# Lightning attention, a Fourier mix and an MLP on one core: two planner costs raised, behind a norm and behind a fold

## The chip, the cores and the metric

The kernel runs on one core of a Trainium2 chip. The metric is the device time of one execution in microseconds; the time of a kernel is the median of several runs on the chip. A profiled execution is recorded apart, and its times of single instructions are quoted here with the line of the kernel that issued them (L644 is line 644).

## The reference

Four batches of 768 tokens, eight heads of 64, so 512 features. Causal linear attention with a decay per head, in blocks, is followed by a Fourier mix over tokens and features, a layer norm, and an MLP of 512 to 2048 to 512. All is float32.

```python
intra = einsum('bhic,bhjc->bhij', qb, kb) * Dmask
out[:, :, sl] = einsum('bhij,bhjd->bhid', intra, vb) + einsum('bhid,bhde->bhie', qb * lam_pow, kv_state)
kv_state = lam_block * kv_state + einsum('bhsd,bhse->bhde', kb * rev_pow, vb)
...
x = attention.transpose(0, 2, 1, 3).reshape(4, 768, 512)
u = x + real(fft(fft(x, axis=1), axis=2))
un = (u - mean(u)) / sqrt(var(u) + 1e-6)
return u + relu(un @ w_ch1) @ w_ch2
```

## The kernel before

**Groups.** A batch is six tiles of 128 tokens. The Fourier mix is symmetric, so tile t is always finished with its mirror tile t + 3; such a pair is a group (b, g), 256 tokens. There are twelve groups in the order `ORDER`: for each batch g = 1, 2, 0. The first four, (0,1), (0,2), (0,0) and (1,1), are `PLAIN`: their MLP is computed directly. The other eight are `LATE`; they are taken in pairs by a scheme with fewer products (`late`, L891 and on), which begins when everything else is done, at about 425 us, and runs to the end.

**The front work of a batch.** `attn(b)` goes through six chunks of 128 tokens. Each loads k, q and v (L265, queue of SyncE), transposes k and q on TensorE (L276, L281), forms the scores (L300), masks them with the decay on VectorE (L304), updates the state (L320, L322), forms the output (L335, L341) and turns it back (L357); ScalarE empties that turn in two copies (L361, L362). The rows needed in mirrored order are written to DRAM (L376 for the last ones, on ScalarE's queue) and gathered back by GpSimd (L448, L461). Then `fft_ln(b)` does the mix. `fold_a` and `fold_b` add and subtract mirrored rows and columns on VectorE (L435 to L439, then L479 to L493); the token transform follows on TensorE (L525, the first of which is pinned to its place in the program), then for each t = 1, 2, 0 the feature transform (`width`, L537 to L542), its assembly on VectorE (L607 to L611) and `norm`: statistics on VectorE (L554, L555), two small operations on GpSimd (L558, L559), the normalised tokens `un` on VectorE (L572). For a plain group TensorE transposes `un` into `ut` (L577); for a late group VectorE transposes it (L585) and it is stored in DRAM (L589), with the unnormalised tokens (L595).

**The other work.** `mlp` is cut into chunks: for each of the 16 column blocks `fc` four matmuls of 256 columns (L644), each a pair of records in the trace, into one of three PSUM banks `pm`, and a ReLU that frees the bank. The ReLU stands on ScalarE (L652), but in the second half of the blocks every odd one stands on VectorE (L650). Behind the blocks come the matmuls of 512 columns of the second layer (L658), and their sums with the tokens (L665 to L670 on VectorE). `half[0]` holds the first eight blocks of the first three plain groups, `half[1]` the other eight; the fourth plain group is one `mlp` of all sixteen. The conversion of the weights from 8-byte words (`load_weights`, L211 to L227) is a third kind of work, and the sums of weights for the late stage (`combine_weights`, L709 on VectorE) a fourth.

**What sets the order.** All pieces are generators that yield an estimated cost. `weave(lead, other, ratio)` takes a piece of the lead, adds its cost, and then takes pieces of the other work until their costs reach `ratio` times the lead's. The front work is the lead and MLP blocks are the other work. So the number that a front piece yields sets how much other work is written behind it in the program; a scheduler then orders each engine's instructions, and each engine runs its own list in that order. When `fft_ln` of the fourth batch is done, what is left of the MLP of (1,1) is woven with the sums of weights, and then the late stage starts with `inputs(0)` (L792 to L798), which stands behind the MLP's last sums in VectorE's list.

```python
def weave(lead, other, ratio):
    t_lead = t_other = 0.0
    for d in lead:
        t_lead += d
        while t_other < t_lead * ratio:
            d = next(other, None)
...
run(weave(fr, back, (t_back - t_half) / (t_rest - t_rest * t_half / t_back)))
...
load_u(0, nc.scalar)
run(weave(combine_weights(0), back, 1.5))
run(back)
```

`LEADS` is (0,): the first batch's mix is written in single pieces, and the branch of `fft_ln` that runs the folds as a whole, with a fixed cost behind each, serves batches 1, 2 and 3.

Of the kernel before, what the change touches and what calls it, by code (L numbers as in the profile page):

```python
# [76 lines left out]
def kernel(  # L77
# [61 lines left out]
    def new(pool, shape, tag, **kw):  # L139
        cnt[0] += 1  # L140
        return pool.tile(shape, F32, tag=tag, name=f"{tag}{cnt[0]}", **kw)

    def psum_a(shape):
        return new(pa, shape, "pa")
# [112 lines left out]
    LEADS = (0,)  # L257
# [207 lines left out]
    def fold_a(b):  # L465
        for a, n in enumerate(BLK):
            yield from fold_x(b, a, n, 1, eo[b][a][1][0:n, 1, 0:DM], xn_[b, HC + a][0:n])
# [32 lines left out]
    def fft_ln(b):  # L500
        sets = []

        def piece(a, i, n):

            c0 = W + QM if i == 4 else QM * (i % 2)
            return sets[a][i in (2, 3)][0:BLK[a], n, c0:c0 + QM]

        if b in LEADS:
            yield from fold_a(b)
            yield from fold_b(b, sets)  # L510
            yield 2.0
        else:
            yield 1.0
            run(fold_a(b))
            yield 6.0 if b - 1 in LEADS else 3.0
            run(fold_b(b, sets))
            yield 12.0 if b - 1 in LEADS else 9.0


        for i in range(5):  # L520
            ps = psum_a([128, 2, NK])
            m = 128 if i < 4 else 1
            for n in range(2):
                for a, rows in enumerate(BLK):
                    mm = nc.tensor.matmul(ps[:, n, :], lhsT=piece(a, i, n), rhs=cs[0:rows, a, i in (2, 3), n, :],  # L525
                                          start=(a == 0), stop=(a == 1))
                    if i + n + a == 0:
                        tc.keep_in_program_order(mm)
            nc.scalar.copy(ys[i][0:m, 0:2 * NK].rearrange("p (k n) -> p n k", n=2), ps[0:m])
            yield 1.4  # L530


        def width(t, ps, only_a):
            y = [ys[i][:, S // 2:S // 2 + 1].broadcast_to([128, 128]) if only_a else ys[i][:, 128 * t:128 * t + 128] for i in range(5)]
            mm = nc.tensor.matmul
            if not only_a:
                mm(ps[:, HM + QM:DM], lhsT=y[2], rhs=dt[:, 2, 0:QM], start=True, stop=True)  # L537
            mm(ps[:, HM:HM + QM + 1], lhsT=y[0], rhs=dt[:, 0, :], start=True, stop=False)
            mm(ps[:, HM:HM + QM + 1], lhsT=y[4], rhs=dt[:, 4, :], start=False, stop=True)
            mm(ps[:, 0:QM], lhsT=y[1], rhs=dt[:, 1, 0:QM], start=True, stop=True)  # L540
            if not only_a:
                mm(ps[:, QM:HM], lhsT=y[3], rhs=dt[:, 3, 0:QM], start=True, stop=True)  # L542

        def even_odd(t):
            return t.rearrange("p (m r) -> p r m", r=2)

        def halves(t):
            return t.rearrange("p (r k) -> p r k", r=2)

        def norm(g):  # L550
            mv = new(np_, [128, G, 2], "mv")
            for i in range(G):
                stt = new(np_, [128, 6], "stt")
                nc.vector.bn_stats(stt, xs[b, TT[g][i]])  # L554
                nc.vector.bn_aggr(mv[:, i, :], stt)  # L555
            ve = new(np_, [128, G], "ve")
            rs = new(np_, [128, G], "rs")
            nc.gpsimd.tensor_scalar(ve, mv[:, :, 1], EPS, None, op0=ALU.add)  # L558
            nc.gpsimd.tensor_tensor(rs, ve, mhalf, op=ALU.pow)  # L559

            yield 9.0 if (b, g) == PLAIN[0] else 1.0
            plain = (b, g) in PLAIN
            if plain:
                ut = uts[b, g] = new(up, [128, KO, G * 128], "ut")
            else:

                to = utd[b, g] = dram.tile([128, KO, G * 128], F32, name=f"utd{b}{g}")
            for i in range(G):
                un = new(np_, [128, DM], "un", bufs=1)
                u = xs[b, TT[g][i]]  # L570
                for o, x in ((un[:, 0:HM], u[:, 0:HM]), (un[:, HM:DM], u[:, DM - 1:HM - 1:-1])):
                    nc.vector.tensor_scalar(o, x, mv[:, i, 0:1], rs[:, i:i + 1],  # L572
                                            op0=ALU.subtract, op1=ALU.mult)
                if plain:
                    pt = psum_a([128, KO, 128])
                    for c in range(KO):
                        mm = nc.tensor.transpose(pt[:, c, :], un[:, 128 * c:128 * c + 128], ident)  # L577
                        if (b, g, i, c) == (*PLAIN[0], 0, 0):

                            tc.keep_in_program_order(mm)  # L580
                    nc.scalar.copy(ut[:, :, 128 * i:128 * i + 128], pt)
                else:

                    uq = new(ep, [128, DM], "e")
                    nc.vector.transpose(uq, un)  # L585
                    for r in range(0, 128, 32):
                        dst = to[:, :, 128 * i + r:128 * i + r + 32].rearrange("(a d) c n -> d c a n", d=32)
                        src = uq[r:r + 32].rearrange("p (c a n) -> p c a n", c=KO, n=32)
                        nc.sync.dma_start(dst, src)  # L589
                yield 0.7  # L590
            if plain:
                return
            for T in TT[g]:
                ud[b, T] = dram.tile([128, DM], F32, name=f"ud{b}{T}")
                nc.sync.dma_start(ud[b, T], xs.pop((b, T)))  # L595

        for t in (1, 2, 0):
            ps = psum_a([128, DM])
            width(t, ps, False)

            A = halves(ps)[:, ::-1, 0:QM]
            B = bs[t % 2]
            nc.scalar.copy(B[:, 1:HM:2], ps[:, QM:HM])
            nc.scalar.copy(B[:, 2:HM:2], ps[:, HM + QM + 1:DM])
            ds = new(fp, [128, 2 * (HM + 2)], "ds")
            nc.scalar.copy(ds[:, HM:2 * HM + 2:HM + 1], ps[:, HM + QM:HM + QM + 1].broadcast_to([128, 2]))
            nc.vector.tensor_tensor(even_odd(ds[:, 0:HM]), A, even_odd(B[:, :]), op=ALU.subtract)  # L607
            nc.vector.tensor_tensor(even_odd(ds[:, HM + 1:2 * HM + 1]), A, even_odd(B[:, :]), op=ALU.add)
            u, v_ = xs[b, t], xs[b, HC + t]
            nc.vector.tensor_tensor(halves(u), halves(u), halves(ds)[:, :, 0:HM], op=ALU.add)  # L610
            nc.vector.tensor_tensor(halves(v_), halves(v_), halves(ds[:, 1:DM + 1])[:, ::-1, :], op=ALU.add)  # L611
            yield 1.6
            if t == 0:
                ps = psum_a([128, DM])
                width(HC, ps, True)
                x3 = xn_.pop((b, HC))
                nc.vector.tensor_tensor(even_odd(v_[0:1, 0:HM]), halves(ps[0:1])[:, ::-1, 0:QM],
                                        even_odd(x3[0:1, 0:HM]), op=ALU.add)
                nc.vector.tensor_tensor(v_[0:1, HM:DM:2], ps[0:1, 0:QM], x3[0:1, HM:DM:2], op=ALU.add)
                nc.vector.tensor_tensor(v_[0:1, HM + 1:DM:2], ps[0:1, HM + 1:HM + QM + 1],  # L620
                                        x3[0:1, HM + 1:DM:2], op=ALU.add)
                yield 0.9
            yield from norm(t)
# [3 lines left out]
    PLAIN, LATE = ORDER[:4], ORDER[4:]  # L627
# [543 lines left out]
    def front(b):  # L1171
        yield from attn(b)
        yield from fft_ln(b)
# [15 lines left out]
    def run(gen):  # L1189
        return sum(gen)  # L1190
# [18 lines left out]
    def beside(lead, t, other, t_other):  # L1209
        return weave(lead, part(other, t_other), t_other / t)  # L1210

    att1, mix = attn(1), fft_ln(0)
    att0 = attn(0)
    run(part(att0, 2.7))
# [4 lines left out]

    half = [[mlp(b, g, h * FO // 2, (h + 1) * FO // 2) for b, g in PLAIN[:3]] for h in range(2)]  # L1220
    fr = chain([att1, fft_ln(1)] + [front(b) for b in range(2, B)])
    t_rest, t_back = 3 * t_front - 5 * t_chunk, len(PLAIN) * t_mlp - 50.0
    t_half = 1.5 * t_mlp
# [49 lines left out]
```

## Time and profile before

| | us |
|---|---|
| median of 3 runs | 794.67 (794.67 to 795.24) |
| profiled execution | 796.12 |
| its span | 793.9 |
| TensorE idle in the span, 0 to 103 | 15.4 |
| 103 to 148 | 2.1 |
| 148 to 258 | 1.0 |
| 258 to 366 | 3.5 |
| 366 to 428 | 0.3 |
| 428 to the end | 8.2 |

The rows of idle time are the width of a stretch less TensorE's busy time in it, from the table of windows. The stretch from 103 to 428 us is the one in which front work and MLP are woven; the late stage is the last. In the profile a group of like instructions stands on one line: start, duration, engine, line, operation, output and inputs by the program's names, shape, number of records, and in brackets the idle time before it with what ended it. The granted clock is full (1.00) in every one of these stretches but the last two, 0.97 from 366 to 428 and 0.99 after.

### The profile page before, as it was taken

The page shows a single profiled execution, that of the slowest core. Times are in us where ns is not written, and L with a number is a line of the kernel's source. Part 1 is how long each engine was busy: PE and PEld are TensorE (multiplying, and loading weights), DVE is VectorE, ACT ScalarE, POOL GpSimd, SP SyncE. Part 2 cuts the span into 40 slices and gives each one's busy share as a digit, 9 for nine tenths or more (in the row PEclk, how much of TensorE's full clock was granted, in tenths as well). Part 3 has the DMA queues.
Part 4 walks back from the last instruction along what each step waited for, and adds up shares of the span by engine and source line. Part 5 has one row for each costly group of instructions (what it writes and reads, how often), then busy time and mean ns, then how long its engine had stood idle before and what let it go on. Part 6 is the DMA issues. An engine that isn't in the chain of part 4 may idle for free.

```text
span 793.9 us, 14617 instructions
## 1 busy us (share of the span) xinstructions
PE 763.4 (96%) x5616; PEld 646.3 (81%) x5616; DVE 585.5 (74%) x1148; ACT 225.4 (28%) x532; POOL 197.6 (25%) x198
## 2 busy tenths in 40 slices
PE   6889989999999999998999999999999999999995
PEld 5768766758585867767946889988999999999995
DVE  6899889675844582345698998769966699758983
ACT  3665443335621221321201221022211342034300
POOL 3223330011111110211004950279205001220021
PEclk9999999999999999999999999999999999999998
DMA  9978723238842147441233374345944455455341
GB/s 243 247 165 245 196 85 129 85 74 205 227 116 77 54 79 146 108 143 64 54 66 107 133 246 162 97 167 191 348 147 153 150 174 185 129 176 186 121 131 70
DMA packets 152331, 116.80 MB, mean 147 GB/s; under 512 B 113998, under 2 KB 113998, under 8 KB 152262
## 3 DMA queue, kind: packets, MB, share of 16 engines
q1 hardware_dynamic: 147120, 103.39, 45.8%
q0 software_dynamic: 2112, 6.69, 2.4%
q10 hardware_dynamic: 3030, 5.78, 2.0%
q8 instruction: 45, 0.74, 0.4%
q14 instruction: 24, 0.20, 0.1%
HBM read 83.58 MB, written 32.25 MB: 146 GB/s over the span
## 4 chain that ended last, share of the span: by engine, by line
PE 78%; DVE 9%; DMA 4%; issue 4%; ACT 1%; POOL 1%; SPq 0%; POOLq 0%; ACTq 0%; DVEq 0%
PE p L1046 21%; PE p L891 12%; PE p L976 11%; PE pm L658 10%; PE pm L644 9%; PE pa L525 3%; PE pa L300 3%; PE pa L341 3%; DMA x<-xb,ix 2%; PE pa L335 2%; PE pa L276 1%; PE pa L357 1%; PE pa L320 1%; DVE sc L304 1%; PE pa L281 1%
## 5 line engine op out<-in xcount | busy, mean ns | idle before, releaser
L644 PE MATMUL pm<-ut,w 128*128 128x256 f32 x512 | 119.7, 384 | 0.0
L658 PE MATMUL pm<-w,hr 128*128 128x512 f32 x256 | 115.7, 596 | 0.2 <-DVE w L227 0.2
L644 PEld LDWEIGHTS pm<-ut,w 128*128 128x128 f32 x512 | 95.6, 192 | 14.2 <-issue 2.1
L658 PEld LDWEIGHTS pm<-w,hr 128*128 128x128 f32 x256 | 46.6, 190 | 49.3 <-issue 48.0
L1060 POOL TENSOR_TENSOR y<-y,u 128x512 f32<-128x512 f32 x12 | 18.8, 1569 | 199.2 <-DVE y L1069 156.8
L1046 PE MATMUL p<-tx,sx 128*128 128x128 f32 x416 | 54.9, 275 | 0.0
L1046 PEld LDWEIGHTS p<-tx,sx 128*128 128x128 f32 x416 | 50.6, 192 | 0.0
L891 PE MATMUL p<-ur,w 128*128 128x256 f32 x192 | 46.9, 379 | 0.1
L272 POOL TENSOR_TENSOR kd<-k,decay 128x512 f32<-128x512 f32 x20 | 22.0, 1100 | 95.3 <-PE pa L320 48.7
L1052 ACT COPY y<-p 128x128 f32<-128x128 f32 x48 | 12.8, 266 | 104.1 <-PE p L1046 103.8
L1054 DVE TENSOR_TENSOR y<-p,y 128x128 f32<-128x128 f32 x92 | 25.5, 286 | 22.5 <-PE p L1046 15.9
L891 PEld LDWEIGHTS p<-ur,w 128*128 128x128 f32 x192 | 36.3, 190 | 5.7 <-issue 0.5
L304 DVE TENSOR_TENSOR sc<-pa,decay 128x512 f32<-128x512 f32 x48 | 31.5, 683 | 8.1 <-PE pa L300 7.9
L1046 PE MATMUL p<-w,ha 128*128 128x128 f32 x288 | 37.4, 275 | 0.0
L300 PEld LDWEIGHTS pa<-qT,kT 64*128 64x128 f32 x384 | 26.1, 193 | 13.4 <-ACT qT L283 7.4
L652 ACT ACTIVATE hr<-pm 128x256 f32<-128x256 f32 x44 | 16.7, 385 | 66.2 <-PE pm L644 66.0
L1046 PEld LDWEIGHTS p<-w,ha 128*128 128x128 f32 x288 | 35.0, 192 | 0.2
L300 PE MATMUL pa<-qT,kT 64*128 64x128 f32 x384 | 30.8, 292 | 3.3 <-ACT qT L283 3.1
L341 PE MATMUL pa<-sc,v 128*64 128x128 f32 x384 | 30.0, 279 | 4.0 <-DVE sc L304 3.8
L558 POOL TENSOR_SCALAR ve<-mv 128x2 f32<-128x2 f32 x12 | 3.4, 286 | 122.3 <-DVE mv L555 122.3
L891 PE MATMUL p<-sx,w1s 128*128 128x256 f32 x128 | 32.9, 380 | 0.2 <-DVE sx L794 0.2
L650 DVE TENSOR_SCALAR hr<-pm 128x256 f32<-128x256 f32 x20 | 8.3, 414 | 32.8 <-PE pm L644 32.8
(234 smaller groups left out, 1736.6 us busy)
## 6 DMA issues: line engine op xcount, KB each, us to landing
tx<-td SPq DMA_DIRECT2D x84, 256.0 KB, 2.7
raw<-in_moe_w_ch_dram SPq DMA_DIRECT2D x32, 512.0 KB, 4.0
tx<-sd SPq DMA_DIRECT2D x42, 256.0 KB, 2.7
sd<-tx SPq DMA_DIRECT2D x28, 256.0 KB, 2.1
k<-in_k_dram SPq DMA_DIRECT2D x24, 256.0 KB, 5.2
q<-in_q_dram SPq DMA_DIRECT2D x24, 256.0 KB, 4.3
v<-in_v_dram SPq DMA_DIRECT2D x24, 256.0 KB, 5.0
td<-tx SPq DMA_DIRECT2D x21, 256.0 KB, 2.0
```

The source lines that it names most:

```text
L272: nc.gpsimd.tensor_tensor(kd, kt, kpow, op=ALU.mult)
L300: mm(pss[hi][:, hp, :], lhsT=kT[HD[hi], hp, :], rhs=qT[HD[hi], hp, :], start=True, stop=True)
L304: nc.vector.tensor_tensor(t, pss[hi], decay[:, hi::2, :], op=ALU.mult)
L341: mm(po[HD[hi], hp, :], lhsT=vt[:, 2 * hp + hi, :], rhs=sc[hi][:, hp, :], start=(c == 0 and hp == 0), stop=(hp == HP - 1), skip_group_chec ...
L525: mm = nc.tensor.matmul(ps[:, n, :], lhsT=piece(a, i, n), rhs=cs[0:rows, a, i in (2, 3), n, :], start=(a == 0), stop=(a == 1))
L644: nc.tensor.matmul(ps, lhsT=w1[:, c, 128 * fc:128 * fc + 128], rhs=ut[:, c, :], start=(c == 0), stop=(c == KO - 1))
L658: nc.tensor.matmul(ps, lhsT=hr[(fc - f0) // 4][:, fc % 4, 128 * i:128 * i + 128], rhs=w2[:, fc, :], start=(fc == f0), stop=(fc == f1 - 1))
L891: nc.tensor.matmul(ps, lhsT=s2.A[a][:, kt, 128 * i:128 * i + 128], rhs=U[b][:, kt, :], start=(first and kt == 0), stop=(kt == 1), skip_gro ...
L976: nc.tensor.matmul(ps[:, 128 * i:128 * i + 128], lhsT=ab[m][0][:, 128 * i:128 * i + 128], rhs=ab[m][1], start=(start and i == 0), stop=Tru ...
L1046: nc.tensor.matmul(ps[:, 0:HM // 2], lhsT=ab[m][0][i], rhs=ab[m][1][:, i, :], start=(start and i == 0), stop=(i == HF // 2 - 1), skip_grou ...
L1054: V.tensor_tensor(o, ps[:, 0:HM // 2], o, op=ADD)
L1060: nc.gpsimd.tensor_tensor(o, y, u, op=ADD)
```

## The change

Two of the yielded costs are changed, and nothing else. In `fft_ln`, the cost behind `fold_b` is raised from 9.0 to 11.5 for the batches that are not below `LATE[-1][0]`, which is 3: so for batch 3 alone. Batch 1 keeps 12.0 and batch 2 keeps 9.0. In `norm`, the cost between the statistics and the normalised tokens is raised from 1.0 to 3.0 for the plain groups other than the first, that is (0,2), (0,0) and (1,1). The line that sets `plain` moves up since the new cost uses it.

```diff
             run(fold_b(b, sets))
-            yield 12.0 if b - 1 in LEADS else 9.0
+            yield 12.0 if b - 1 in LEADS else 9.0 if b < LATE[-1][0] else 11.5
...
-            yield 9.0 if (b, g) == PLAIN[0] else 1.0
             plain = (b, g) in PLAIN
+            yield 9.0 if (b, g) == PLAIN[0] else 3.0 if plain else 1.0
             if plain:
                 ut = uts[b, g] = new(up, [128, KO, G * 128], "ut")
```

## The prediction

> **What bounds the kernel now.** I read the busy table first, then the timeline of TensorE for its idle places, then, around each of those that the change can reach, the timeline of VectorE and the chain of waits, and last the TensorE windows of 1 us, for the granted clock.
>
> ```profile
> span 793.9 us, 14617 instructions
> PE 763.4 (96%) x5616; PEld 646.3 (81%) x5616; DVE 585.5 (74%) x1148; ACT 225.4 (28%) x532; POOL 197.6 (25%) x198
> 147.16 0.76 PE L577 MATMUL pa<-ident,un 128*128 128x128 f32 x4 [0.94 <-DVE un L572]
> 176.14 1.69 PE L300 MATMUL pa<-qT,kT 64*128 64x128 f32 x16
> 257.72 0.90 PE L525 MATMUL pa<-cs,fe 128*128 128x193 f32 x4 [0.98 <-DVE fe L484]
> 292.07 1.09 PE L341 MATMUL pa<-sc,v 128*64 128x128 f32 x16 [1.23 <-DVE sc L304]
> 365.64 0.59 PE L525 MATMUL pa<-cs,fe 128*128 128x193 f32 x2 [2.04 <-DVE fe L484]
> 427.76 1.10 PE L891 MATMUL p<-sx,w1s 128*128 128x256 f32 x4 [0.22 <-DVE sx L794]
> ```
>
> TensorE is busy 96% of the span, so only its 30.5 us of idle (793.9 - 763.4) and its clock can be won without removing work. The number in brackets is the idle time before the group and what ended it. The reader is to see that every one of these waits on VectorE, at a seam between two batches, and that the largest is at the fourth batch's folds (365.64). There the windows give a second cost (columns: width, busy and matmuls, granted clock, DMA share, GB/s):
>
> ```profile
> 365.00:366.00 1.00, 0.36 (x2) 1.00 0.00 0
> 366.00:367.00 1.00, 1.00 (x5) 0.56 0.00 0
> 367.00:368.00 1.00, 1.00 (x4) 0.50 0.06 16
> 368.00:369.00 1.00, 1.00 (x4) 0.50 0.00 0
> 369.00:370.00 1.00, 1.00 (x4) 0.73 0.00 0
> 370.00:371.00 1.00, 1.00 (x6) 1.00 0.00 0
> ```
>
> After the 2.04 us hole the clock is halved: 0.44 + 0.50 + 0.50 + 0.27 = 1.71 us of work lost. So this seam costs 2.04 + 1.71 = 3.75 us, and the second edit aims at it. What ends its wait is in the chain:
>
> ```profile
> 353.11 0.33 ACTq L376
> 353.47 5.60 DMA ur<-utd
> 359.11 3.13 DMA x<-xb,ix
> 362.26 0.69 DVE fe L435
> 365.64 0.59 PE pa L525 x2
> ```
>
> The write of the last rows to DRAM (issued on ScalarE's queue at L376, behind the 2 MB load of `ur`), the gather of their mirror, and VectorE's fold from 362.26 to 365.58.
>
> **What the Trainium skill says.** "TensorE: Matmul & The Clock Gate", Part 1, "What's actually happening": the clock is either half or full, decided by how busy TensorE was in a free-running window of about 3.4 us. The trace agrees in the value (0.50) and in the length (366.1 to 369.5); which gap tips it depends on where the window falls: here 2.04 us did, 1.23 and 0.98 did not. The same page, "Architectural detail", on queue depths: ScalarE and VectorE take their instructions strictly in order; the trace shows nothing against it, and the fold step below rests on it. "Trainium Kernel Development and Optimization", "Key Constraints": DMAs from the SP, ACT and POOL queues share the same 16 DMA engines; the trace agrees, the write of 353.47 needing 5.60 us beside the `ur` load on one queue.
>
> **The change part by part.** No instruction is added or removed. Only the costs told to the planner change, so I compared the order of each engine's instructions in the two built programs. They differ between the seam at 147 us and the start of the late stage at 427 us; POOL's order and all that comes after is unchanged, and the norms of groups (0,2) and (0,0) do not move, so of the three groups of the first edit only (1,1) is touched. A TensorE instruction of L644 takes 0.43 us (a chunk of 4 is 1.73), one of L658 0.86: two trace records each, 3.60 us for 8 records and so on.
>
> *Norm of (1,1), 147.16.* One more L644 stands before the transposes: the hole shrinks by 0.43, from 0.94 to 0.51. Two further L644 and a swap of L644 by L658 follow at places without a hole: 0. Sum -0.43.
>
> *Batch 2, chunks 1 and 2.* The scores L300 took 1.69 us (176.14) and 1.58 (193.92) where an undisturbed group takes 1.16: a wait inside the group, for a bank that ScalarE (L362) has not emptied. In the new order there is an L658 (0.86) between L357 and L300 of chunk 2, and chunk 1's first wait is for a VectorE instruction long done. That gives 0 to -0.53 and 0 to -0.42; the trace names ScalarE for the weight loads of L300, so I take nearly all: -0.50 and -0.44.
>
> *SP's queue.* One more weight piece (L211) is issued ahead of chunk 2's k, q, v; it waits for its buffer until about 179 us, so k goes out near 180 instead of 178.62. With the 5.2 us that this load takes in the list of DMA issues, and q and v behind it, they land by about 189.4 and are needed at 191. Cost 0, cover 1.6 us; bounds 0 to +1.5 if these loads take twice their median.
>
> *Batch 2, folds, 257.72.* Four L644 instead of eight stand between the last L357 and the sixteen L658. But the gather L461 waits for L670, which ends those L658: the chain L658, L670, gather, fold hangs on TensorE's own work, and the L525 behind it moves along. 0; bounds -0.3 to +0.3, as the landing of the gather varies.
>
> *Batch 3, chunk 0, 292.07.* The products L537 to L542 of batch 2's second and third groups come 1.3 to 1.7 us later in TensorE's order, so VectorE's norm work ahead of L304 is later too. I follow its queue: L304 (2 x 0.64) starts at about 291.0 instead of 290.74, +0.26. The hole becomes 1.5; bounds 0 to +0.8, since I can't tell how much of the delay its own slack takes.
>
> *Batch 3, folds, 365.64.* This is what the second edit does: L357 is preceded by 2 instead of 3 L658, so the whole chain starts 0.86 us earlier, and behind it stand 4 L658 and then 24 L644 instead of 18. Counted from the start of L357, TensorE has work for 0.44 + 4 x 0.86 + 5 x 1.73 = 12.53 us before it comes to the sixth chunk (12.68, since the like stretch of before, 352.23 to 363.60, took 0.15 more than its sum); the fold's end is at 13.79 (365.58 - 351.79), the same as before. What else is late: chunk 5 needs a `pm` bank, of which there are three, and that bank is freed by L650, the ReLU of chunk 1, on VectorE. In the old order this L650 ran at 359.32, ahead of the fold; in the new one it is queued behind nine of the fold's instructions (L435 to L489), like the second L650 at 366.17 now. So it starts at 366.17 - 351.79 = 14.38 and ends at 14.80, and TensorE resumes 0.06 later, as it does behind the fold now: a hole of 14.86 - 12.68 = 2.18, in front of L644 instead of L525. The hole has changed its place, +0.14, and I leave the half clock behind it as it was (1.71). Bounds: -1.85 if the clock's window falls so that it isn't halved, +0.5 if the landing is later.
>
> *Start of the late stage, 427.76.* Work moved forward is missing behind. After the first L537 group of batch 3 the new order has 8 more L644 ahead (3.46 us), so the VectorE chain that begins with L607 at 381.88 and ends with the sums of weights (L709, end 423.52) is 3.46 later against TensorE, minus one L650 (0.33) that no longer stands in it: +3.13. It holds no idle time but the turns over POOL that belong to it. Its slack:
>
> ```profile
> 418.90 4.62 DVE L709 TENSOR_TENSOR w<-w 128x1024 f32<-128x1024 f32 x4
> 425.54 0.42 DVE L669 TENSOR_TENSOR y<-pm,x 128x256 f32<-128x256 f32 x1 [2.02 <-PE pm L658]
> ```
>
> 2.02 us. VectorE becomes late by 3.13 - 2.02 = 1.11, and so do L669, L670, L792 and L794, for which L891 waits: 0.22 becomes 1.33, +1.11. Bounds 0 to +1.6.
>
> Sum: -0.43 - 0.50 - 0.44 + 0.26 + 0.14 + 1.11 = +0.14. The profiled execution took 796.12 (793.9 of span and 2.2 around it), which gives 796.26; it lies 1.45 above the median of the runs (794.67), so the forecast is 794.8.
>
> **The rivals.**
>
> 1. *Slower: the clock at 292 us.* If the hole in front of L341 grows from 1.23 past the point at which the clock is halved, somewhere between 1.23 and 2.04 by this trace, 1.71 is lost there, on top of the sum: +1.85, 796.5. For it: 1.5 is my middle, and 2.0 its upper bound. Against it: a window may split the hole, and the 0.26 is small beside the 0.81 that lies between the two known gaps. The late start at its +1.6 would add 0.5.
>
> 2. *Faster: the fold's hole is filled or doesn't cost the clock.* If L650 came out ahead of the fold, because its product is ready before the gather lands, TensorE would have 14.4 us of work for 13.8 of waiting and lose neither hole nor clock: -2.04 - 1.71 in place of +0.14, 790.9. Against it: the queue's order is fixed when the program is built. The milder form, the hole stays but not the half clock, gives 0.14 - 1.71 = -1.57, 793.1. For it only that the window runs freely.
>
> 3. *Slower: k, q, v of chunk 2.* If the piece ahead waits longer for its buffer than to 179, TensorE stands at 191: each us past a slack of 1.6 costs one. At +4 it is 0.14 + 2.4, 797.2. Against: this buffer's readers end at 179 in the trace of before.
>
> **How the numbers follow.** What can be told from no change is 0.2%, 1.6 us. The forecast with its own range (793.6 to 796.0) has 0.50. Rival 1 has 0.28, rival 3 0.05, and other late work, mainly the late stage above its bound, 0.04. Rival 2 in both forms has 0.13. Of the 0.37 in the late cases some 0.02 stay within the bound, so that a median above 796.26 (794.67 and 0.2%) has 0.35, one below 793.08 has 0.13, and 0.52 lies between. The range from 793.0 to 797.6 reaches the milder form of rival 2 and the first rival with its additions, and leaves about 0.1 out at either end.
>
> **What would show it.** Right: L577's hole at 0.5; L300 of chunks 1 and 2 at 1.2; a hole of about 2.2 now in front of an L644 that waits for L650, with half clock behind it; L891 waiting 1.3 for L794. Wrong: no hole near 366 or full clock there (rival 2), a clock below 1.00 near 293 (rival 1), L276 or L281 waiting for a DMA near 191 (rival 3).

## The result, and the profile after

| kernel | runs | median us | ratio to before, 95% interval |
|---|---|---|---|
| before | 12 | 795.27 | |
| changed | 12 | 798.06 | 1.0046 [1.0025, 1.0068] |

The change makes the kernel slower by 0.46%, beyond the 0.2% that can be told and above the range of the forecast (793.0 to 797.6). The profiled execution took 797.13 us (span 794.9), 0.9 below the median of its kernel, while that of before lay above its own; it shows where the time goes, not how much of it.

TensorE's timeline in the changed kernel, at the places that the prediction went through (start, duration, instruction, idle time before it and what ended it):

```profile
147.41 0.77 PE L577 MATMUL pa<-ident,un 128*128 128x128 f32 x4 [0.51 <-DVE un L572]
177.21 1.26 PE L300 MATMUL pa<-qT,kT 64*128 64x128 f32 x16
185.46 8.04 PE L644 MATMUL pm<-ut,w 128*128 128x256 f32 x36 [0.98 <-ACT hr L652]
257.69 0.90 PE L525 MATMUL pa<-cs,fe 128*128 128x193 f32 x4 [1.17 <-DVE fe L484]
292.23 1.09 PE L341 MATMUL pa<-sc,v 128*64 128x128 f32 x16 [1.80 <-DVE sc L304]
366.44 1.99 PE L644 MATMUL pm<-ut,w 128*128 128x256 f32 x8 [1.62 <-DVE hr L650]
423.71 1.89 PE L891 MATMUL p<-ur,w 128*128 128x256 f32 x8
428.77 1.10 PE L891 MATMUL p<-sx,w1s 128*128 128x256 f32 x4 [3.17 <-DVE sx L794]
```

Most lines are those foretold: 0.51 at the norm, shorter scores, and at 366 a hole in front of L644 that waits for L650. Two are not. At 185 a hole of 0.98 is new. And the hole at the start of the late stage, 0.22 before and 1.33 in the forecast, is 3.17. TensorE reaches that stage 1.63 us earlier than before (423.71 against 425.34) and leaves the hole 1.01 us later (428.77 against 427.76). The windows show the clock behind both large holes:

```profile
366.00:367.00 1.00, 0.56 (x3) 1.00 0.00 0
...
429.00:430.00 1.00, 1.00 (x6) 0.93 0.62 238
430.00:431.00 1.00, 1.00 (x4) 0.50 0.07 25
431.00:432.00 1.00, 1.00 (x4) 0.50 0.06 16
432.00:433.00 1.00, 1.00 (x4) 0.50 0.00 0
433.00:434.00 1.00, 1.00 (x6) 0.86 0.00 0
```

In this execution the half clock is gone at 366 and stands at 430 instead, 0.07 + 3 x 0.50 + 0.14 = 1.71 us again. What holds VectorE there is in its timeline and in SyncE's queue:

```profile
420.52 4.62 DVE L709 TENSOR_TENSOR w<-w 128x1024 f32<-128x1024 f32 x4
426.54 0.42 DVE L669 TENSOR_TENSOR y<-pm,x 128x256 f32<-128x256 f32 x1 [1.40 <-DMA out_dram<-y]
```

```profile
422.15 1.10 SPq L595 DMA_DIRECT2D ud<-x  x2
423.35 0.39 SPq L631 DMA_DIRECT2D out_dram<-y  x1
```

The weight sums end at 425.14, about as late as foretold. Then L669 stands 1.40 us more: it writes the only `y` buffer, whose store (L631) is queued on SyncE behind the stores of the last norm (L589, L595). In the kernel before, TensorE's start of the late stage and the issue of that store were:

```profile
425.34 2.21 PE L891 MATMUL p<-ur,w 128*128 128x256 f32 x8
421.72 0.40 SPq L631 DMA_DIRECT2D out_dram<-y  x1
```

### The profile page after: what moved, and what is told of

Its sections match the earlier page's. It is cut to its first block, busy times and chain, and to the rows that moved or that the text cites. A ratio compares the mean times of both kernels' runs of the same rounds, so it can differ in the third digit from the quotient of the medians.

```text
span 794.9 us, 14623 instructions
## 1 busy us (share of the span) xinstructions
PE 762.8 (96%) x5616; PEld 646.6 (81%) x5616; DVE 582.6 (73%) x1148; ACT 224.1 (28%) x532; POOL 196.5 (25%) x198
## 4 chain that ended last, share of the span: by engine, by line
PE 73%; DVE 13%; DMA 5%; issue 4%; ACT 2%; POOL 1%; SPq 1%; POOLq 0%; ACTq 0%; DVEq 0%
PE p L1046 21%; PE p L891 12%; PE p L976 11%; PE pm L644 7%; PE pm L658 6%; PE pa L341 3%; PE pa L525 3%; PE pa L300 2%; DMA x<-xb,ix 2%; PE pa L335 2%; DVE stt L554 1%; PE pa L276 1%; PE pa L320 1%; DVE sc L304 1%; DVE un L572 1%
## 5 line engine op out<-in xcount | busy, mean ns | idle before, releaser
L644 PE MATMUL pm<-ut,w 128*128 128x256 f32 x512 | 118.1, 381 | 2.6 <-DVE hr L650 1.6
L644 PEld LDWEIGHTS pm<-ut,w 128*128 128x128 f32 x512 | 94.7, 190 | 16.5 <-DVE hr L650 2.0
L891 PE MATMUL p<-ur,w 128*128 128x256 f32 x192 | 47.6, 384 | 0.0
L1054 DVE TENSOR_TENSOR y<-p,y 128x128 f32<-128x128 f32 x92 | 25.5, 285 | 22.6 <-PE p L1046 16.0
L891 PEld LDWEIGHTS p<-ur,w 128*128 128x128 f32 x192 | 37.0, 193 | 5.6 <-issue 0.5
L891 PE MATMUL p<-sx,w1s 128*128 128x256 f32 x128 | 33.8, 388 | 3.2 <-DVE sx L794 3.2
L650 DVE TENSOR_SCALAR hr<-pm 128x256 f32<-128x256 f32 x20 | 8.3, 415 | 36.0 <-PE pm L644 36.0
L652 ACT ACTIVATE hr<-pm 128x256 f32<-128x256 f32 x44 | 16.7, 384 | 60.0 <-PE pm L644 59.8
```

Of the source, the lines that this page charges most:

```text
L644: nc.tensor.matmul(ps, lhsT=w1[:, c, 128 * fc:128 * fc + 128], rhs=ut[:, c, :], start=(c == 0), stop=(c == KO - 1))
L891: nc.tensor.matmul(ps, lhsT=s2.A[a][:, kt, 128 * i:128 * i + 128], rhs=U[b][:, kt, :], start=(first and kt == 0), stop=(kt == 1), skip_gro ...
L1054: V.tensor_tensor(o, ps[:, 0:HM // 2], o, op=ADD)
```

## Experiments

Single executions of one kernel differ by several us, so each kernel ran 6 to 22 times beside the kernel before on the same chip, and two sums are formed. Each run comes with its span and mean granted clock; (1 - clock) x span, averaged over the runs, is called the clock lost, and the run's time less it the rest. About 1 to 2 us of the clock lost lie in the tail, where TensorE has ended, and cost nothing (2.25 in the profiled execution of before, 1.6 in that of the changed kernel). A run's clock is recorded in steps of 0.001, which are 0.8 us, so the division of one run is good to about 1 us. The second figures are standard errors.

| kernel | runs | ratio [95%] | clock lost | rest |
|---|---|---|---|---|
| changed | 12 | 1.0046 [1.0025, 1.0068] | 4.99 ± 0.63 | 794.2 |
| before, beside 1 to 4 | 58 | | 2.93 ± 0.20 | 793.2 |
| 1 norm edit alone | 14 | 1.0003 [0.9982, 1.0023] | 2.56 ± 0.45 | 793.4 |
| 2 fold edit alone | 22 | 0.9998 [0.9985, 1.0011] | 2.45 ± 0.22 | 793.5 |
| 3 own buffer for last y | 13 | 1.0036 [1.0016, 1.0055] | 4.66 ± 0.63 | 793.9 |
| 4 and sums meant for later | 22 | 1.0018 [1.0003, 1.0034] | 4.27 ± 0.36 | 793.6 |
| before, beside 5 to 8 | 38 | | 2.91 ± 0.22 | 793.1 |
| 5 changed, again | 9 | 1.0055 [1.0031, 1.0079] | 4.70 ± 0.53 | 795.0 |
| 6 sums pinned later | 22 | 1.0022 [1.0008, 1.0036] | 2.68 ± 0.39 | 794.9 |
| 7 late hole put into before | 11 | 1.0047 [1.0027, 1.0068] | 4.57 ± 0.50 | 795.2 |
| 8 two ReLUs on ScalarE | 9 | 1.0044 [1.0018, 1.0070] | 4.87 ± 0.62 | 794.0 |
| before, beside 13 to 15 | 51 | | 3.05 ± 0.22 | 792.8 |
| 13 products put ahead | 22 | 1.0005 [0.9990, 1.0020] | 2.57 ± 0.35 | 793.6 |
| 14 load of ur later, in before | 14 | 0.9994 [0.9980, 1.0008] | 2.72 ± 0.33 | 792.3 |
| 15 both, in changed | 22 | 0.9991 [0.9975, 1.0006] | 3.39 ± 0.35 | 791.7 |

Runs 9 to 12 are told below.

**1, 2: one edit at a time.** The kernel before with one of the two lines of the diff.

> Only the cost in norm is raised (3.0). Theory 1 (the late start decides: each edit moves one chunk of four L644 from behind the last norm to before it, 1.73 us, and the last y has to wait for the store of the y before it, whose slack in the kernel before I put at about 0.65): the hole before L891 is about 1.3 us, that at the fold about 1.2 to 1.8, those at 185 and 292 as in the changed kernel (0.98, 1.80); ratio to before 0.999 to 1.003. Theory 2 (the norm edit's holes at 185 and 292 and a halved clock behind them decide): ratio as for both edits, 1.003 to 1.006, with runs near 801.

> Only the cost behind the fourth batch's folds is raised (11.5). Theory 1: again one chunk, so the hole before L891 is about 1.3, the fold's about 1.2, nothing at 185 and 1.23 at 292 as in the kernel before; ratio 0.998 to 1.002. Theory 2: no cost in this kernel, ratio at or below 1.000 and no hole above 0.4 before L891.

Alone, neither shows a cost (both intervals hold 1); together they cost 0.46%. In TensorE's order each edit takes four L644 from behind the fourth batch's first group of products L537 (32 of them before, 28 with either, 24 with both). The late holes, in TensorE's timeline of run 1:

```profile
427.45 1.10 PE L891 MATMUL p<-ur,w 128*128 128x256 f32 x4 [1.16 <-DVE y L670]
428.77 1.10 PE L891 MATMUL p<-sx,w1s 128*128 128x256 f32 x4 [0.22 <-DVE sx L794]
```

and of run 2:

```profile
427.26 1.10 PE L891 MATMUL p<-sx,w1s 128*128 128x256 f32 x4 [0.54 <-DVE sx L794]
```

That is 1.38 together in run 1, and 0.54 in run 2, where about 1.3 was expected, in place of 3.17: there is a slack that one chunk about uses up and two exceed. Run 1 also has the 0.98 at 185 and the 1.81 at 292, so these belong to the norm edit, and its ratio shows no cost of theirs. At the fold it missed: holes of 2.23 and 0.41, where 1.2 to 1.8 was expected.

**3, 4: VectorE's two delays at the late stage.** In the changed kernel the last `y` goes to a free buffer, and then half of the last weight sums behind `inputs(0)`.

```diff
-                y = new(up, [128, DM], "y", bufs=1)
+                y = new(up, [128, DM], "y", bufs=1) if (b, T) != (1, 4) else new(up, [128, KO, G * 128], "ut").rearrange("p c n -> p (c n)")[:, 0:DM]
...
-            todo = [(a21, a11, a21, SUB), (b12, b22, b12, SUB)]
+            todo = [(a21, a11, a21, SUB)] if part == 1 else [(b12, b22, b12, SUB)]
...
-                    run(inputs(0))
+                    run(inputs(0)); run(combine_weights(2))
```

> The changed kernel, with the very last y in a free ut buffer, so that L669 need not wait for the store of the y before. Theory 1: L669 no longer waits for a DMA, the hole before L891 falls from 3.17 to about 1.8 (VectorE's chain ends 425.14 in the changed kernel's trace, 1.40 before L669 starts); 1.4 us faster than the changed kernel, more if the clock stays whole there. Theory 2: the hole shrinks too but runs near 801 stay as frequent, and the median moves by no more than 0.5.

> The same, and the half of the last weight sums that only the second layer needs (2.3 us of VectorE) is put behind inputs(0). Theory 1: VectorE is early again, the hole before L891 is at most 0.6 and the clock behind it whole; 2.6 to 4.5 us faster than the changed kernel, at or below the kernel before (0.995 to 1.000), with no runs near 801. Theory 2: the median stays within 1 us of the changed kernel's less 1.4, because the holes at 185 and 292 are untouched.

VectorE's timeline in run 3, with no wait left ahead of L669:

```profile
428.12 0.42 DVE L669 TENSOR_TENSOR ut<-pm,x 128x256 f32<-128x256 f32 x1
```

The hole went from 3.17 to 1.90: the store held 1.3 of it, and most of the rest is VectorE's chain. In run 4 the scheduler left the second half of the sums where they had been, so the hole was 1.90 again, and run 4 repeats run 3. In both the clock lost stays high, and neither's time can be told from the changed kernel's: the 1.4 us that run 3 was to gain are not shown. The revised theory: the late hole costs its idle time and, in many executions, a window of half clock behind it.

**5 to 8: is it that hole?** The changed kernel again; the same as run 4 with the sums pinned behind `inputs(0)`; the kernel before with a hole made there, by four more operations on VectorE that change no value; and, for the hole at 366, two ReLUs moved to ScalarE.

```diff
# 6, beside the edits of 4
-                V.tensor_tensor(o[:, i:i + n // 2], x[:, i:i + n // 2], y[:, i:i + n // 2], op=op)
+                pin = tc.keep_in_program_order if part == 2 else lambda z: z; pin(V.tensor_tensor(o[:, i:i + n // 2], x[:, i:i + n // 2], y[:, i:i + n // 2], op=op))
# 7, in the kernel before
-            todo = [(a21, a11, a21, SUB), (b12, b22, b12, SUB)]
+            todo = [(a21, a11, a21, SUB), (b12, b22, b12, SUB), (wz[:, 0], wz[:, 0], wz[:, 0], ALU.max), (wz[:, 1], wz[:, 1], wz[:, 1], ALU.max)]
# 8, in the changed kernel
-            if fc % 2 and f1 == FO:
+            if fc % 2 and f1 == FO and (f0, fc) not in ((0, 1), (0, 3)):
```

> The changed kernel unaltered, beside the others on the same chip. Theory 1 (revised: the idle of the late start adds about 1 us by itself, and the rest of the slowdown is half clock that this hole brings on): holes of about 1.8 at 292, 1.6 to 2.3 at 366 and 3.2 before L891; over its runs about 2 us more of clock lost than in the kernel before (4.99 against 2.93 so far) and about 1 us more of the rest. Theory 2 (the clock is lost at 292 or 366, wherever the holes there are wide): the same figures.

> The changed kernel with the last y in a free ut buffer and the second-layer half of the last weight sums pinned behind inputs(0), so that VectorE is early at the late start (the run before this left those sums ahead of L669). Theory 1: the hole before L891 is at most 0.6, the clock lost falls back to about 3 us a run, and the kernel is at the level of the kernel before (0.998 to 1.002), 2 to 3.5 us faster than the changed kernel beside it. Theory 2: the holes at 292 and 366 are untouched, so the clock lost stays at 4.3 to 5 us a run and no more than 1.5 us is gained.

> The kernel before with four more operations of 1.15 us each on VectorE (the maximum of parts of w2s with themselves) behind the last weight sums, and nothing else. Theory 1: VectorE is 4.6 - 2.0 = 2.6 us late, the hole before L891 about 2.8, and the runs slow down as in the changed kernel: about +2 of idle and +1 to +2 of clock lost, ratio 1.003 to 1.005. Theory 2: only the idle comes, about +2, and the clock lost stays at 2.9 a run.

> The changed kernel with the ReLU of blocks 1 and 3 of the fourth plain group on ScalarE, so that no L650 stands behind the fourth batch's fold. If the hole at 366 in front of L644 is L650's place in VectorE's order, it goes, and a hole of 1 to 2 us appears later, before the L525 that needs the second block's fold. Theory 1: the median moves by less than 1 us. Theory 2: the clock lost falls by 1 us or more.

Run 7 decides between the two. The kernel before, with nothing but a late VectorE at that point, becomes as slow as the changed kernel (1.0047), and its clock lost rises by 1.66. TensorE's timeline there, and the windows behind the hole:

```profile
429.81 1.10 PE L891 MATMUL p<-ur,w 128*128 128x256 f32 x4 [2.50 <-DVE y L670]
```

```profile
430.00:431.00 1.00, 0.91 (x4) 0.92 0.00 0
431.00:432.00 1.00, 0.87 (x2) 0.50 0.25 94
432.00:433.00 1.00, 1.00 (x4) 0.50 0.44 168
```

Run 6 is the counterpart: with 1.26 left of the hole, where 0.6 was expected, the clock lost is back at the level of before. The rest is not, since the displaced sums cost 0.24 and 0.94 of idle at 463 and 470, in front of L891. In run 5's profiled execution the hole is 3.14 and the clock stays whole behind it: the hole makes half clock likely, not certain. The profiled executions agree with the means. Runs 9 to 12 aside, six have a late hole of 1.9 to 3.2 us, and in four of them a stretch of half clock stands there (the changed kernel, runs 4, 7 and 8, not 3 and 5); seven have one of 1.4 or less, and none of them has it.

The traces also show what decides it. In the kernel before, half clock begins at 366.13 and, at the end of the kernel, at 789.38: 423.25 us apart, which is 124 times 3.413. In the changed kernel it begins at 429.86 and 791.67, 106 times 3.413 apart, and the stretches in the other traces fit such a grid too. Every trace has the stretch at the end, so it fixes the windows of 3.413 us in each execution, and TensorE's busy time in them can be read. Here are the window ahead of the changed kernel's half clock, and the two that share the hole of run 5:

```profile
426.44:429.86 3.42, 1.09 (x5) 1.00 0.14 54
...
424.10:427.51 3.41, 1.63 (x8) 1.00 0.43 156
427.51:430.93 3.42, 2.06 (x10) 1.00 0.20 77
```

The changed kernel's 3.17 puts 2.3 us of idle into one window; run 5's 3.14 is split into 1.8 and 1.4. From 97 us on, in all 17 traces, 13 windows at full clock are followed by half clock, and TensorE was idle for 1.81 us or more in each. The other 3398 are not, and none of them was idle for more than 1.81. So a hole costs clock when about 1.8 us of idle fall into one window, and where the windows lie is chance. If they lie evenly, a hole of 3.17 brings on half clock in an estimated 87% of executions, one of 1.9 in half of them, and one below 1.8 in none. Ahead of 97 us the rule is less sharp: two windows with 1.49 and 1.75 were followed by half clock too.

Run 8 has the hole at 366 where it was expected, in front of the second block's L525, so L650's place in the queue did make it:

```profile
370.16 2.56 PE L525 MATMUL pa<-cs,fe 65*128 65x193 f32 x14 [2.23 <-DVE fe L484]
```

The hole is wider than the 1 to 2 us expected, and no gain in time is shown.

**9 to 12: the sums on GpSimd.** The last weight sums on GpSimd, idle there, with the free `y` buffer: in the changed kernel (9), in the kernel before (10), and in the kernel before with the two ReLUs moved and the cost behind the fourth fold at 15 (11) and 17 (12).

```diff
-                V.tensor_tensor(o[:, i:i + n // 2], x[:, i:i + n // 2], y[:, i:i + n // 2], op=op)
+                (V if part == 0 else nc.gpsimd).tensor_tensor(o[:, i:i + n // 2], x[:, i:i + n // 2], y[:, i:i + n // 2], op=op)
```

> The changed kernel with the last y in a free ut buffer and the last two weight sums (combine_weights part 1, 4.6 us of VectorE) on GpSimd, which is idle there. Theory 1: VectorE's chain before the late start is 4.6 us shorter, the hole before L891 at most 0.4 and nothing new in the first layer; clock lost about 2.7 a run, the rest 1.3 us below the last version's, so the ratio to before is 0.999 to 1.001: both edits without the late hole are worth about nothing. Theory 2: still slower by 0.2% or more, with the holes at 185 and 292.

> The same two repairs on the kernel before, with its costs. Theory 1: the hole before L891 was 0.22 there, so nothing is won: ratio 0.999 to 1.001. If it is faster by more, the repairs help elsewhere too, and a_pool is to be read against this kernel.

> The kernel before with those repairs, the ReLU of blocks 1 and 3 of the fourth plain group on ScalarE, and the cost behind the fourth batch's folds at 15 instead of 9 (norm left alone): 28 L644 ahead of the first L525 instead of 18, TensorE has work for 16.1 us of the 18.3 to 18.7 that both folds take. Theory 1: the hole of 2.0 at 366 becomes one or two of together at most 1.5, none above 0.5 before L891, less clock lost; ratio 0.996 to 0.999, the fastest so far.

> The same with 17: 32 L644 ahead of the first L525, work for 17.9 us, but four L644 more are gone behind the last norm. Theory 1: the fold's hole is below 0.5; VectorE is 6.9 us late against 6.6 of slack at the late start, so a hole of up to 0.6 before L891; ratio 0.995 to 0.999.

All four missed badly: 1.0118 [1.0092, 1.0143], 1.0125 [1.0085, 1.0166], 1.0189 [1.0161, 1.0217] and 1.0171 [1.0143, 1.0198]. VectorE's timeline in run 9 shows why:

```profile
421.87 3.86 DVE L572 TENSOR_SCALAR un<-x,mv,rs 128x256 f32<-128x256 f32 x2
...
435.11 0.69 DVE L792 TENSOR_TENSOR sx<-ur 128x512 f32<-128x512 f32 x1 [3.25 <-DMA ud<-x]
```

The sums on GpSimd beside that L572, and the same L572 in the changed kernel:

```profile
420.02 5.56 POOL L709 TENSOR_TENSOR w<-w 128x1024 f32<-128x1024 f32 x2 [5.28 <-DVE w2s L709]
414.42 0.71 DVE L572 TENSOR_SCALAR un<-x,mv,rs 128x256 f32<-128x256 f32 x2
```

A pair of L572 that takes 0.71 in the changed kernel takes 3.86 while GpSimd works on its sums, and two of VectorE's own sums beside the earlier pair took 3.37 and 2.74 where others take 1.2. So the last norm ends late, its stores (L595) leave late, and L792 waits 3.25 for one of them, because its buffer lies where the tokens `x` lay. The hole before L891 was 7.55 in run 9. The Trainium skill has the reason ("SBUF — State Buffer", "SBUF: two separate sides"): VectorE and GpSimd share a port pair as an exclusive lock, which is held for a whole instruction. The trace agrees: the two L572 end at 423.38 and 425.73, each about 0.15 us after a GpSimd sum (423.22 and 425.58). What the wider fold costs are worth in time can't be judged from runs 11 and 12. In their traces the hole at 366 is 1.93 in run 11 and gone in run 12, so that enough moved work does fill it, with 9.2 and 12.6 us of idle before L891 in these two kernels.

**13 to 15: the two edits without the late hole, and what holds the fold.** In run 13, beside the free `y` buffer, the first two products of block 1 are issued ahead of the product that waits for L794; nothing is added to VectorE. In run 14 the load of `ur` is pinned to its place in the program. Run 15 has all of it. The repair of run 13 was not tried on the kernel before, whose late hole is only 0.22.

```diff
# 13: what began block i (X: a11 b11, Y: a12 b21, their copy, sum and ReLU) becomes begin(i)
+            if i == 0:
+                begun = [begin(n) for n in range(2 if j == 0 else 1)]
+            elif i > 1 or j:
+                begun = [None] * i + [begin(i)]
+            X, Z = begun[i]
# 14
-            queue.dma_start(r[:, h], utd[b, g])
+            load = queue.dma_start(r[:, h], utd[b, g]); j or tc.keep_in_program_order(load)
```

> The changed kernel with the last y in a free ut buffer and, in the first late layer of the first pair, the first two products of block 1 (eight more records, 1.9 us) issued ahead of the product that waits for L794. Theory 1: the hole before the first L891 with sx falls from 3.17 to at most 1.0 in all, clock lost about 2.8 a run, ratio to before 0.999 to 1.002: without the late hole the two edits are worth nothing either way. If it stays at 1.003 or more, the holes at 185 and 292 are what costs.

> The kernel before, with the 2 MB load of ur (L759, on ScalarE's queue) pinned to its place in the program, so that it is issued at about 395 us instead of just ahead of the write of the last rows (L376). If that write lands late because of the load (5.60 us now, 2.5 to 3 for others), the fold starts about 2.5 to 3 us earlier: the hole of 2.04 at 366 goes to at most 0.3 (one of up to 1 us may come before the second block's L525), clock lost falls by 0.5 to 1 us a run, ratio 0.995 to 0.998. If other work is what lacks, nothing changes.

> Both in the changed kernel. If both readings hold, the hole at 366 is gone and at most 1.0 is left before L891: ratio 0.996 to 1.000, above b_ur's by the holes at 185 and 292 (about 1 us).

TensorE's timeline in run 13, where the hole used to be:

```profile
427.09 1.97 PE L891 MATMUL p<-ur,w 128*128 128x256 f32 x8 [0.34 <-DVE ut L670]
```

With 0.34 in place of 3.17 both edits together are neutral (1.0005), although the holes at 185, 292 and 366 are all still there. In run 14 the chain of waits at the fold has the write of the last rows in 2.06 us:

```profile
356.42 2.06 DMA xb<-xn
```

In the kernel before it took 5.2 us: it was issued at 353.11, and GpSimd's wait for it (L461) ended at 358.3. The 5.60 that the prediction gives it stands on a line that names another transfer, `ur<-utd`: the second half of the load, issued at 353.47 right behind the write.

From the start of L357 to the end of the first L484 it takes 10.75 us in run 14 and 13.79 before. The hole of 2.04 is gone, and one of 0.95 stands before the second block's L525. So what the second edit set out to fill is made by a load issued around the write; whether the shared queue delays the write, or the load's traffic as such, is not separated. In run 15, 0.50 is left near 366 and 0.34 at the late start. In time 14 and 15 can't be told from before, their intervals holding 1, and the gain expected of run 14 (0.995 to 0.998) is not shown. In the rest they lie 0.6 and 1.2 below, with a standard error of 0.3 and 0.2, but 0.4 of each lies outside the profiled span (time less span is 1.85 in both and 2.23 before). Run 15 is clearly below the changed kernel; that it is below the kernel before is not shown.

## Why the prediction was wrong

*The step that failed* is "Start of the late stage". It took VectorE's idle time of 2.02 as the slack and came to 1.33. VectorE's chain came about as computed (its weight sums end 3.25 later against TensorE, for 3.13), but a second wait had less slack: L669 needs the store of the `y` before. That store was issued at 421.72 in the kernel before. With the 3.19 from issue to L669's start that the changed kernel shows (423.35 to 426.54), it would have landed at 424.9, an estimated 0.6 before L669. Being queued behind the last norm's stores it moves with the norm: against TensorE's first L891 its issue moved from 3.62 ahead to 0.36 ahead, 3.26 later. So L669 starts 2.63 later against TensorE, and the eight L891 ahead of the hole took 1.89 instead of 2.21, so that TensorE came to it 0.32 sooner; together that is the 2.95 by which the hole grew. Without that store (run 3) 1.90 is left; of what is above 1.33, 0.2 is an L915 that comes in between L792 and L794, and 0.3 the same eight L891. The term was +1.11 and is +2.95. The prediction had followed SyncE's queue at 178 us and not here.

*The term that was missing* is the clock behind this hole. The rival priced half clock rightly (1.71) but put it at 292, where 1.80 of idle costs nothing that the means show: runs 1 and 13 have it and lose no more clock than before. It can happen there: the profiled executions of runs 3 and 9 have half clock from 293.4 on, the other eight with that hole don't. Its 1.8 us are just what a window needs. At the late stage it costs 1.7 to 2 us a run on average (run 7 against before, run 5 against 6). By the profiled execution the forecast's +0.14 becomes: late hole +1.84, half clock behind it +1.71, the new hole at 185 +0.98, that at 292 +0.31, batch 2's folds +0.39, and the fourth batch's fold -2.27 (0.42 less idle where 0.14 more was expected, and no half clock), in all +3.1. Of this, where the half clock fell and the 0.42 are chance. VectorE's last instruction (L1054) starts 2.68 later than before, 788.45 against 785.77, so 0.4 of the sum is not accounted for; the medians differ by 2.8, and the ratio makes it 3.7. That the span grew by only 1.0 comes from the last stores, which ended sooner after it.

*Right*: the norm (0.51); the scores of chunks 1 and 2 (1.26 and 1.16; -0.43 and -0.42 for -0.50 and -0.44); no wait for k, q, v; the fold's hole in front of L644, made by L650 (run 8). Its size too: 1.6 to 2.3 in the seven profiled executions that have both edits and nothing else changed at this fold, 1.6 to 2.0 in three with the fold order of before (before, runs 7 and 10), so the edits moved the hole and did not fill it. *Within its bounds*: 1.80 at 292, taken as 1.5; batch 2's first fold hole, +0.2 for 0 (its second, 0.18 before and 0.38 now, was not in the forecast). *Overlooked*: 185 us, where three L652 come to stand behind L338 and L344 on ScalarE and the next chunk has no bank.

Rival 2, a gain at the fold, did not come, though in the profiled execution its milder form did happen there: the half clock was lost elsewhere instead. Rival 3 didn't happen. What stays open is how often half clock fell at each place: the windows can be laid only over the profiled executions, and the other runs give a mean clock alone.

## What to carry to other kernels

When other work is moved forward to fill a hole, ask what it covered where it came from, and take as the slack the least over all that the exposed instruction waits for, a store that frees its buffer included, on whichever queue it stands. Two shifts that are each free can cost together once their sum passes that slack, so they are to be tried alone and together. And before filling a hole, follow the chain that makes it: here one load, issued elsewhere, took away more of the hole than the second edit's moved work, though no gain in time is shown.

## What the runs showed of the hardware

- Half clock came in windows of 3.413 us that keep one grid through an execution. From 97 us on, such a window followed a window at full clock just when TensorE was idle in that one for about 1.8 us (1.81 or more in 13 windows, at most 1.81 in 3398 others). So 3.14 us split over two windows left the clock whole (run 5), and 1.81 in one window halved it (run 3, at 293). One execution can't price a hole; over 9 to 58 runs a kernel's mean clock loss is known to 0.2 to 0.6 us.
- VectorE's L572 pair went from 0.71 to 3.86 us beside GpSimd sums, and a sum of 128x1024 that VectorE does in 1.16 us took 2.4 to 3.3 on GpSimd (6.48 and 5.56 for two).
- A 256 KB write landed in 2.06 us without the load of `ur` (run 14), and in 5.2 (before) and 4.4 (changed kernel) when issued between the two halves of that load on its queue. The load is two of 512 KB by the list of DMA issues, so 1 MB, and not 2 MB as the prediction and an expectation have it.
